# One q load per batch, queries in a permuted order inside blocks, and transposes on halves of the TensorE array

## The chip, the cores and the metric

The kernel runs on one core of a Trainium2 chip. The metric is the device time of one execution in microseconds; the runs shown give a median. A separate profiled execution gives the trace: what each engine (PE = TensorE, ACT = ScalarE, DVE = VectorE, POOL = GpSimd, SP = SyncE) did when, and what it waited for.

## The reference

Two steps, for 8 batches, 8 heads, 576 tokens and head size 64. First an attention over a window of 128 tokens with a distance bias per head, then a token mixer on its output:

```
scores = q @ k.T / 8 ; rel = i - j
scores = where(0 <= rel < 128, scores - slope[h] * |rel|, -1e9)      # slope[h] = 2 ** -(h + 1)
x = softmax(scores) @ v                                    # to [8, 576, 512]
wq, wk = x @ w_q, x @ w_k                                  # [8, 576, 64]
mixed = (wq @ wk.T / 8) @ x
out = maximum(mixed, 0) @ w_out                            # float32
```

Inputs and output are float32; the kernel works in float16 with float32 sums.

## The kernel before, in words

A batch's 576 tokens are four blocks of 128 and a tail of 64. For a batch b the work is made of named operations, and every operation's engine, its place and its PSUM bank are written out in one long text, `ORDER`, in which each word is an operation with its engine (`MUL0.1.0:D`, `XT0.0:P21`). The engines run their own operations in the order of that text. Nothing is planned at run time.

* `Lq`, `Lk`, `Lv` (lines 363 and 380) are loads on POOL's queue that cast to float16; one load is a block of 128 tokens of all heads, in pieces of 256 bytes of float32. `Lt` (line 370) loads the tails of q and k for two batches. The first blocks of batch 0 come over the SP and ACT queues as float32 (`LF`, line 400). `Lw` and `Lwo` load the weights over SP's queue (lines 440 and 448), released by a small DVE operation `wz`.
* `TQ` transposes q and k of a block together on PE (line 234), eight transposes of 128 by 128 into one bank; `ETQ` copies the bank to `qkT`. `TT` and `ETT` do it for the tails.
* `QK` makes the scores of one key block for four heads, in a pair of banks; `EXP` (ACT, line 587) takes the exponential, `MUL` (DVE, line 594) multiplies by the exponential of the bias, a constant tile that also holds the mask. For the last key block, whose queries are 192 + 64 columns, there is a second tile `biasl`.
* `PV` multiplies by v with a column of ones, so that the sums come along; `RC` (line 648) takes the reciprocal and `X` (line 634) scales to x. `PV.4`, `RC.4`, `X.4` are the tail of 64 queries.
* `XT`, `EXT` transpose x and copy it to `xT`; `XTT`, `EXTT` the tails. For each two batches follow `WK`, `WT`, `WQ` (the projections), `G` (wk.T @ x), `MX` with `RM` (mixed, and the relu, lines 770 and 772), and nine output blocks: `OUT`, a copy `EO`, and `DO`, the transfer on SP's queue (lines 832 and 835).

Attention of later batches and the mixer of earlier ones are interleaved by the text. PSUM is four pairs of banks; an operation takes a pair or one bank of it, and holds it until its copy is done. Copies go to ACT (line 238) or DVE (line 240), as the text says. Line 231 is the helper of all matmuls. `WM` are matmuls on zeros at the start.

Of the kernel before, what the change touches and what calls it, by code (L numbers as in the profile page):

```python
# [25 lines left out]
NNAT = 4  # L26
NV = 4
NPT = 5
PTW = 1088
# [4 lines left out]
OSB = 12  # L34
WIDE = ()

WARM = (12, 3, 4, 3, 3, 5,)

ORDER = """
warm:D LF0.0.1.0:A ident:G LF0.0.1.1:A LF0.1.0.1:S ones:D LF0.1.0.0:S Lk0.1:G LF0.0.0.1:S  # L40
LF0.0.0.0:S Lq0.2:G pads:D zeros:D Lt0:G WM.0:P31 TF0.1.1:P00 idh:D TF0.1.0:P01 iota:G Lk0.2:G
wmc:D WM.1:P31 TF0.0.1:P10 EF0.1.0:D EF0.1.1:D mask:G TF0.0.0:P01 EF0.0.1:A Lq0.3:G bias:A
EF0.0.0:D Lk0.3:G WM.2:P31 TJ0.2.0:P00 TJ0.1.1:P01 EJ0.2.0:D QK0.0.1:P1 Lq1.1:G EJ0.1.1:D
QK0.1.1:P0 QK0.0.0:P2 Lv0.0:G EXP0.1.1:A biasl:D TT0:P30 Lq1.2:G TJ0.2.1:P31 EXP0.0.0:A
QK0.1.0:P0 Lk1.1:G EJ0.2.1:D EXP0.0.1:A ETT0:D TJ0.3.0:P31 Lk1.2:G EXP0.1.0:A EJ0.3.0:D ETT1:D
WM.3:P21 TJ0.3.1:P10 Lv0.1:G QK0.2.1:P2 EJ0.3.1:D QK0.2.0:P3 MUL0.1.0:D QK0.3.1:P1 EXP0.2.0:A
Lk1.0:G QK0.3.0:P0 MUL0.0.0:D Lq1.0:G EXP0.2.1:A MUL0.2.0:D MUL0.0.1:D Lk1.3:G EXP0.3.1:A
MUL0.2.1:D PV0.0:P2 Lq1.3:G TQ1.1:P30 EXP0.3.0:A RC0.0:D MUL0.1.1:D TQ1.2:P31 Lv0.2:G ETQ1.1:D
ETQ1.2:A MUL0.3.1:D PV0.1:P0 Lv0.3:G X0.0:D QK1.1.0:P3 Lk2.1:G QK1.1.1:P1 RC0.1:D MUL0.3.0:D
EXP1.1.0:A TQ1.0:P20 Lq2.1:G X0.1:D EXP1.1.1:A ETQ1.0:D XT0.0:P21 Lv1.0:G QK1.0.0:P0 EXT0.0:D  # L50
Lq2.2:G TQ1.3:P20 EXP1.0.0:A MUL1.1.1:D QK1.0.1:P1 PV0.2:P3 Lk2.2:G ETQ1.3:D EXP1.0.1:A
MUL1.0.0:D QK1.2.1:P2 Lv1.1:G QK1.3.1:P0 RC0.2:D EXP1.2.1:A PV0.3:P1 X0.2:D Lq2.3:G RC0.3:D
QK1.2.0:P3 X0.3:D QK1.3.0:P2 Lk2.3:G EXP1.3.0:A MUL1.0.1:D TQ2.1:P10 Lv1.2:G MUL1.1.0:D
EXP1.3.1:A PV1.0:P2 MUL1.2.1:D XT0.1:P11 Lv1.3:G RC1.0:D MUL1.3.0:D EXT0.1:A Lv0.4:G TQ2.2:P00
ETQ2.1:D Lq2.0:G ETQ2.2:A X1.0:D WM.4:P01 PV1.1:P1 MUL1.3.1:D Lv1.4:G EXP1.2.0:A QK2.1.0:P0
QK2.1.1:P2 wz:D RC1.1:D Lw:S Lk2.0:G X1.1:D EXP2.1.0:A TQ2.3:P30 MUL1.2.0:D Lk3.1:G Lwo.1:S
XT1.0:P31 EXP2.1.1:A Lwo.3:S ETQ2.3:D PV1.2:P0 Lt1:G Lwo.2:S PV1.3:P1 EXT1.0:A RC1.2:D Lwo.0:S
X1.2:D PV0.4:P2 RC1.3:D RC0.4:D QK2.2.0:P0 X1.3:D Lq3.1:G EXP2.2.0:A X0.4:D Lk3.0:G WM.5:P30
PV1.4:P1 XT1.1:P31 RC1.4:D X1.4:D QK2.2.1:P0 Lq3.0:G EXT1.1:A XTT0:P30 CWQ:D Lv2.0:G TQ2.0:P10
EXP2.2.1:A EXTT0:D WK0:P31 ETQ2.0:D Lq3.2:G MUL2.1.1:D QK2.0.1:P1 EWK0:A Lk3.2:G QK2.0.0:P0  # L60
MUL2.2.0:D WT0:P30 EXP2.0.1:A WQ0:P31 Lv2.1:G EWT0:D EXP2.0.0:A MUL2.0.1:D G0:P30 CW.1:D EWQ0:A
CW.2:D TT2:P00 MUL2.0.0:D EG0:A Lv2.4:G ETT2:D MX0.4:P3 MX0.1:P1 ETT3:D MX0.0:P2 RMT0:A RM0.1:D
MX0.2:P0 RM1.0:A Lk3.3:G MX0.3:P3 RM0.2:D TQ3.1:P10 RM0.0:A RM0.3:D RM1.2:A Lq3.3:G QK2.3.1:P2
RM1.1:A CW.0:D QK2.3.0:P0 CW.3:D TQ3.0:P30 EXP2.3.1:A Lv2.2:G ETQ3.1:D OUT0.3:P11 ETQ3.0:D
Lk4.2:G EXP2.3.0:A PV2.0:P2 MUL2.1.0:D OUT0.1:P10 Lv3.1:G RM1.3:A RC2.0:D MUL2.3.0:D EO0.3:A
QK3.0.0:P3 Lv2.3:G QK3.0.1:P0 X2.0:D EXP3.0.0:A OUT1.0:P11 MUL2.3.1:D Lv3.0:G EO0.1:A TQ3.2:P20
MUL3.0.0:D OUT0.2:P21 EXP3.0.1:A Lk4.1:G ETQ3.2:D PV2.1:P3 Lq4.2:G EO1.0:A MUL3.0.1:D EO0.2:A
QK3.1.0:P0 QK3.1.1:P1 RC2.1:D Lq4.1:G MUL2.2.1:D EXP3.1.0:A TQ3.3:P20 X2.1:D OUT0.0:P21 Lv3.2:G
EXP3.1.1:A ETQ3.3:D PV2.2:P3 Lq4.0:G MUL3.1.0:D EO0.0:A QK3.2.1:P0 QK3.2.0:P1 RC2.2:D
EXP3.2.1:A Lq4.3:G OUT1.3:P21 X2.2:D MUL3.1.1:D Lv3.3:G EXP3.2.0:A PV2.3:P3 MUL3.2.1:D PV3.0:P0  # L70
OUT1.4:P20 Lk4.3:G EO1.3:A RC2.3:D RC3.0:D X2.3:D Lk4.0:G QK3.3.1:P1 X3.0:D EO1.4:A QK3.3.0:P3
XT2.0:P21 EXP3.3.0:A MUL3.2.0:D Lv3.4:G PV3.1:P0 EXT2.0:D TQ4.2:P20 Lt2:G EXP3.3.1:A MUL3.3.0:D
TQ4.1:P30 XT2.1:P21 RC3.1:D ETQ4.2:A MUL3.3.1:D OUT1.1:P31 Lv4.1:G ETQ4.1:D PV3.2:P1 EXT2.1:D
EO1.1:A Lk5.0:G OUT1.2:P30 RC3.2:D X3.1:D Lv4.0:G PV3.3:P2 X3.2:D EO1.2:A QK4.1.1:P0 Lv4.2:G
RC3.3:D TQ4.3:P30 X3.3:D EXP4.1.1:A QK4.1.0:P1 Lk5.1:G ETQ4.3:D PV2.4:P2 EXP4.1.0:A XT3.0:P31
RC2.4:D TQ4.0:P30 Lq5.0:G X2.4:D EXT3.0:A PV3.4:P0 ETQ4.0:D QK4.2.0:P2 Lq5.1:G XT3.1:P10
RC3.4:D EXP4.2.0:A X3.4:D QK4.2.1:P3 Lq5.3:G TT4:P11 EXT3.1:D EXP4.2.1:A QK4.0.1:P0 Lk5.3:G
XTT2:P20 MUL4.1.1:D WK2:P10 EXP4.0.1:A EXTT2:D Lk5.2:G ETT5:D WT2:P20 ETT4:D EWK2:A Lq5.2:G
MUL4.2.0:D QK4.0.0:P0 QK4.3.1:P3 EWT2:A QK4.3.0:P1 MUL4.2.1:D EXP4.0.0:A WQ2:P21 Lq6.3:G
MUL4.1.0:D EXP4.3.1:A G2:P20 Lv4.3:G MUL4.0.1:D MUL4.0.0:D EWQ2:A Lk6.0:G PV4.2:P3 MUL4.3.1:D  # L80
EG2:A TQ5.1:P21 Lq6.2:G EXP4.3.0:A RC4.2:D X4.2:D MX2.3:P0 TQ5.0:P20 Lv4.4:G RM2.3:A ETQ5.1:D
MX2.0:P3 RM3.3:A Lk6.3:G PV4.1:P1 ETQ5.0:D RM2.0:A MX2.1:P0 MUL4.3.0:D MX2.2:P2 Lk6.2:G RM3.0:A
TQ5.3:P30 RC4.1:D RM2.2:D RM3.2:A TQ5.2:P31 Lq6.0:G RM3.1:A X4.1:D QK5.0.0:P2 ETQ5.2:D Lv5.0:G
EXP5.0.0:A PV4.0:P1 OUT3.3:P01 RC4.0:D ETQ5.3:D Lk6.1:G RM2.1:A QK5.0.1:P2 X4.0:D EO3.3:A
PV4.3:P3 Lq6.1:G MUL5.0.0:D EXP5.0.1:A QK5.2.1:P0 RC4.3:D OUT2.2:P10 Lv5.1:G X4.3:D EXP5.2.1:A
MUL5.0.1:D PV4.4:P2 Lv5.4:G QK5.1.1:P3 EO2.2:A RC4.4:D QK5.1.0:P0 MUL5.2.1:D Lv5.2:G EXP5.1.1:A
XT4.1:P11 DO2.2:S X4.4:D OUT2.0:P10 DO0.3:S Lv5.3:G EXP5.1.0:A EXT4.1:D DO0.1:S TQ6.3:P20 Lt3:G
MUL5.1.1:D DO0.2:S EO2.0:A QK5.3.1:P3 MX2.4:P0 DO1.0:S ETQ6.3:D TQ6.0:P11 EXP5.3.1:A DO0.0:S
TQ6.2:P10 ETQ6.0:D Lq7.1:G RMT2:A QK5.2.0:P2 QK5.3.0:P3 ETQ6.2:D TQ6.1:P11 EXP5.3.0:A Lk7.1:G
MUL5.1.0:D PV5.0:P0 OUT2.1:P10 RC5.0:D EXP5.2.0:A ETQ6.1:D Lk7.0:G PV5.1:P3 X5.0:D Lq7.0:G  # L90
QK6.1.1:P2 EO2.1:A MUL5.2.0:D QK6.0.0:P0 EXP6.1.1:A XT4.0:P11 Lv6.0:G RC5.1:D MUL5.3.1:D
OUT3.0:P10 EXP6.0.0:A X5.1:D Lq7.2:G QK6.0.1:P2 EXT4.0:D QK6.1.0:P3 EXP6.0.1:A XT5.0:P00
MUL5.3.0:D OUT2.3:P11 Lk7.2:G EXT5.0:D EXP6.1.0:A PV5.4:P2 MUL6.0.0:D PV5.2:P0 EO2.3:A RC5.4:D
PV5.3:P3 X5.4:D OUT3.1:P11 EO3.0:A RC5.3:D RC5.2:D X5.3:D QK6.2.1:P2 X5.2:D Lv6.1:G EO3.1:A
QK6.2.0:P3 TT6:P10 EXP6.2.1:A MUL6.1.1:D XTT4:P11 XT5.1:P00 ETT6:D EXP6.2.0:A MUL6.0.1:D
Lk7.3:G OUT3.4:P01 EXT5.1:D QK6.3.0:P3 EXTT4:D QK6.3.1:P2 Lv6.2:G EXP6.3.0:A TQ7.1:P00
MUL6.1.0:D WK4:P11 MUL6.2.0:D Lv6.4:G EXP6.3.1:A MUL6.2.1:D TQ7.0:P30 Lq7.3:G EWK4:A ETQ7.1:D
WT4:P31 WQ4:P20 ETT7:D Lv6.3:G EWT4:A ETQ7.0:D EO3.4:A PV6.0:P1 Lv7.4:G MUL6.3.1:D EWQ4:A
DO3.4:S QK7.0.1:P3 QK7.0.0:P0 RC6.0:D MUL6.3.0:D EXP7.0.1:A DO1.3:S G4:P20 Lv7.0:G DO1.4:S
X6.0:D Lv7.1:G DO1.1:S MUL7.0.1:D TQ7.2:P21 EG4:A DO3.3:S PV6.1:P1 Lv7.3:G EXP7.0.0:A ETQ7.2:D  # L100
DO2.1:S MX4.1:P3 DO1.2:S RC6.1:D QK7.1.1:P2 Lv7.2:G X6.1:D RM5.1:A PV6.2:P0 DO3.0:S EXP7.1.1:A
XT6.0:P31 RC6.2:D X6.2:D MX4.0:P1 RM4.1:A QK7.1.0:P2 EXT6.0:D RM4.0:A MX4.3:P0 TQ7.3:P30
RM5.3:D EXP7.1.0:A OUT3.2:P10 ETQ7.3:D RM4.3:A MX4.2:P2 EO3.2:D RM5.0:A PV6.3:P3 RM4.2:A
MUL7.1.1:D QK7.2.0:P0 RM5.2:A PV6.4:P1 RC6.3:D OUT4.0:P20 X6.3:D EXP7.2.0:A RC6.4:D XT6.1:P21
X6.4:D EO4.0:A MX4.4:P0 QK7.3.1:P3 EXT6.1:D QK7.2.1:P1 RMT4:A DO4.0:S OUT5.1:P20 MUL7.2.0:D
EXP7.2.1:A DO2.0:S DO3.2:S MUL7.1.0:D OUT4.1:P21 EXP7.3.1:A MUL7.0.0:D QK7.3.0:P1 MUL7.2.1:D
EO5.1:A PV7.0:P0 PV7.1:P3 EXP7.3.0:A RC7.0:D DO5.1:S MUL7.3.1:D OUT5.0:P20 DO2.3:S RC7.1:D
EO4.1:A MUL7.3.0:D PV7.2:P1 EO5.0:A X7.1:D OUT5.3:P21 DO5.0:S RC7.2:D X7.2:D PV7.3:P3 EO5.3:A
OUT5.2:P20 X7.0:D RC7.3:D XT7.0:P21 X7.3:D EO5.2:A PV7.4:P0 EXT7.0:D OUT4.3:P10 DO5.2:S RC7.4:D
DO3.1:S X7.4:D XT7.1:P11 EO4.3:A DO4.1:S OUT4.2:P21 EXT7.1:D XTT6:P10 WK6:P11 EXTT6:D WT6:P10  # L110
EWK6:A WQ6:P20 EWT6:A G6:P10 EWQ6:A EO4.2:A OUT5.4:P20 EG6:A DO4.2:S MX6.4:P1 MX6.2:P0 EO5.4:A
MX6.3:P3 RMT6:D RM7.2:A DO5.4:S MX6.0:P2 MX6.1:P1 RM7.3:A DO4.3:S OUT7.4:P01 RM7.1:D RM7.0:A
DO5.3:S RM6.3:A RM6.1:D OUT7.3:P11 EO7.4:A RM6.2:A OUT7.0:P10 DO7.4:S EO7.3:A OUT7.2:P21
# [44 lines left out]
def kernel(  # L158
# [56 lines left out]
    def vtv(b, t):  # L215
        return vt_s[(b // 2) % 2][t][:, b % 2]
# [698 lines left out]
```

## Time and profile before

| what | value |
|---|---|
| median of three runs | 141.13 us (140.97 to 143.18) |
| profiled execution: time | 141.15 us |
| profiled execution: span, first to last instruction | 139.3 us |
| PE, DVE, ACT, POOL busy | 125.9, 114.1, 112.2, 95.6 us |
| granted TensorE clock, mean | 0.987 |
| read from HBM, written | 29.62 MB, 9.44 MB |
| POOL's queue: packets | 109264, 13.77 MB |

A busy time is the union of the engine's instructions; PE's matmuls are pipelined, and their ends are modelled, so a busy PE need not be PE at its peak. A time of the program is 1.8 us longer than the span of its instructions.

### The profile page before, as it was taken

How to read it: one execution, taken by the hardware profiler on the slowest of the kernel's cores; microseconds unless marked ns; L12 is line 12 of the kernel's file. 1: busy time of each engine (PE TensorE's matmuls, PEld its weight loads, DVE VectorE, ACT ScalarE, POOL GpSimd, SP SyncE). 2: the span in 40 equal slices, each digit the busy share in tenths (PEclk: the TensorE clock that was granted, in tenths of full speed). 3: DMA queues.
4: the chain of work that ended last, by engine and by line, in shares of the span. 5: the costliest groups of instructions: out<-in, count | busy, mean ns of one | idle time of the engine just before them, and what ended most of it. 6: DMA issues, size and time to landing. Idle time of an engine off the chain costs nothing.

```text
span 139.3 us, 4479 instructions
## 1 busy us (share of the span) xinstructions
PE 125.9 (90%) x1846; PEld 84.5 (61%) x1846; DVE 114.1 (82%) x254; ACT 112.2 (81%) x165; POOL 95.6 (69%) x118
## 2 busy tenths in 40 slices
PE   6778599879987999999999999999999999999970
PEld 4445486768744566767866477667765656754420
DVE  5657999999996999999999999999998999705000
ACT  3089969898796999868999999978989995279860
POOL 7999999999919999999999999759940000000000
PEclk9999869999999999999999999999999999999999
DMA  4999999999999999999999999999999975505993
GB/s 103 184 155 154 157 153 153 152 150 177 283 184 156 152 155 152 151 153 150 152 151 154 147 172 270 232 202 152 157 171 272 338 274 216 226 5 171 335 355 121
DMA packets 119332, 25.59 MB, mean 184 GB/s; under 512 B 114192, under 2 KB 114192, under 8 KB 119312
## 3 DMA queue, kind: packets, MB, share of 16 engines
q0 software_dynamic: 109264, 13.77, 155.9%
q1 hardware_dynamic: 8992, 11.28, 24.2%
q10 hardware_dynamic: 1056, 0.26, 0.8%
q8 instruction: 14, 0.23, 0.6%
q14 instruction: 6, 0.05, 0.1%
HBM read 29.62 MB, written 9.44 MB: 280 GB/s over the span
## 4 chain that ended last, share of the span: by engine, by line
PE 58%; POOL 22%; DMA 7%; DVE 7%; issue 2%; ACT 1%; ACTq 0%; POOLq 0%
PE pair L231 47%; POOL nat L363 13%; PE pair L234 11%; DMA natt<-in_k_dram 7%; POOL vt L380 6%; DVE pt L594 3%; DVE qkT L240 2%; POOL natt L370 2%; ACT osb L238 1%; DVE x L634 1%; DVE xT L240 0%; DVE rm L772 0%; POOL wm L298 0%; DVE xTt L240 0%; POOL wm L300 0%
## 5 line engine op out<-in xcount | busy, mean ns | idle before, releaser
L587 ACT ACTIVATE pt<-pair 128x1024 f16<-128x1024 f32 x64 | 62.8, 1033 | 4.0 <-PE pair L231 3.6
L380 POOL DMA_DIRECT2D vt<-in_v_dram x40 | 36.9, 976 | 2.6 <-PE pair L231 2.4
L363 POOL DMA_DIRECT2D nat<-in_k_dram x31 | 30.8, 1036 | 3.5 <-DMA nat<-in_k_dram 3.4
L231 PE MATMUL pair<-wout_sb,rm 128*128 128x512 f16 x128 | 31.6, 379 | 0.0
L594 DVE TENSOR_TENSOR pt<-pt,bias 128x1024 f16<-128x1024 f16 x48 | 31.3, 680 | 0.1
L363 POOL DMA_DIRECT2D nat<-in_q_dram x30 | 30.4, 1039 | 0.3 <-DMA vt<-in_v_dram 0.3
L238 ACT COPY osb<-pair 128x512 f32<-128x512 f32 x35 | 20.7, 601 | 7.4 <-PE pair L231 7.2
L231 PEld LDWEIGHTS <-pt 128*128 128x128 f16 x576 | 21.4, 98 | 8.4 <-issue 2.7
L231 PE MATMUL pair<-vt,pt 128*128 128x65 f16 x576 | 24.1, 195 | 2.3 <-ACT pt L587 1.6
L240 DVE COPY qkT<-pair 128x1024 f16<-128x1024 f16 (+1 forms) x38 | 21.7, 591 | 2.6 <-PE pair L231 1.3
L231 PE MATMUL pair<-qkT 64*128 64x256 f16 (+2 forms) x320 | 21.5, 250 | 1.1 <-DVE x L634 0.5
L634 DVE TENSOR_TENSOR x<-pair,inv 128x512 f16<-128x512 f32 x32 | 21.6, 685 | 0.5
L234 PE MATMUL pair<-identh,nat 128*128 128x128 f16 x244 | 19.3, 226 | 1.4 <-ACT pt L587 0.7
L234 PEld LDWEIGHTS <-nat 128*128 128x128 f16 x244 | 15.2, 101 | 5.8 <-issue 3.6
L231 PEld LDWEIGHTS <-rm 128*128 128x128 f16 x128 | 11.1, 97 | 10.6 <-issue 0.8
L231 PEld LDWEIGHTS <-qkT 64*128 64x128 f16 x320 | 11.3, 94 | 7.7 <-issue 3.2
L770 ACT ACTIVATE rm<-pair 128x512 f16<-128x512 f32 x25 | 13.7, 647 | 0.0
L594 DVE TENSOR_TENSOR pt<-pt,biasl 128x1024 f16<-128x1024 f16 x16 | 10.7, 668 | 0.0
L234 PE MATMUL pair<-identh,x 128*128 128x128 f16 x128 | 9.9, 219 | 0.0
L648 DVE RECIPROCAL inv<-pair 128x8 f32<-128x8 f32 (+1 forms) x40 | 7.8, 200 | 1.2 <-PE pair L231 0.8
L234 PEld LDWEIGHTS <-x 128*128 128x128 f16 x128 | 7.6, 98 | 1.7 <-issue 0.8
L240 DVE COPY xT<-pair 128x1024 f16<-128x1024 f16 x12 | 8.2, 687 | 0.4 <-PE pair L234 0.2
(66 smaller groups left out, 116.7 us busy)
## 6 DMA issues: line engine op xcount, KB each, us to landing
out_dram<-osb SPq DMA_DIRECT2D x32, 256.0 KB, 3.0
vt<-in_v_dram POOLq DMA_DIRECT2D x32, 128.0 KB, 5.5
nat<-in_k_dram POOLq DMA_DIRECT2D x31, 128.0 KB, 5.3
nat<-in_q_dram POOLq DMA_DIRECT2D x30, 128.0 KB, 5.1
osb<-in_moe_w_out_dram SPq DMA_DIRECT2D x4, 256.0 KB, 7.2
out_dram<-osb SPq DMA_DIRECT2D x8, 128.0 KB, 3.9
osb<-in_q_dram SPq DMA_DIRECT2D x4, 128.0 KB, 3.8
natt<-in_q_dram POOLq DMA_DIRECT2D x4, 128.0 KB, 7.1
```

The costliest lines, as they stand in the source:

```text
L231: hold(nc.tensor.matmul(*a, **k))
L234: hold(nc.tensor.transpose(*a))
L238: hold(nc.scalar.copy(out_ap, in_ap))
L240: hold(nc.vector.tensor_copy(out=out_ap, in_=in_ap))
L363: return lambda: nc.gpsimd.dma_start(out=natv(b, j, n), in_=(q, k)[j][b, :, P * n:P * n + P, :].transpose([1, 0, 2]))
L370: nc.gpsimd.dma_start(out=natt_s[pr % 2][:, j].rearrange("p e h d -> p (e h) d"), in_=(q, k)[j][2 * pr:2 * pr + 2, :, 512:576, :].rearrang ...
L380: return lambda: nc.gpsimd.dma_start(out=vtv(b, t)[:n, :, 0:D], in_=v[b, :, P * t:P * t + n, :].transpose([1, 0, 2]))
L587: nc.scalar.activation(out=pt[:, 0:1024], in_=two(s.bank).rearrange("p e c -> p (e c)"), func=AF.Exp, scale=SCALE)
L594: ENG2[o.eng].tensor_tensor(out=pt[:, 0:1024], in0=pt[:, 0:1024], in1=bt, op=ALU.mult)
L634: nc.vector.tensor_tensor(out=x[r].rearrange("p (g h d) -> p g h d", g=2, h=4), in0=sums(p)[r, :, :, 0:64], in1=box["inv"][r].unsqueeze(3) ...
L648: nc.vector.reciprocal(out=box["inv"][r], in_=sums(p)[r, :, :, 64])
L770: hold(nc.scalar.activation(out=out_ap, in_=in_ap, func=AF.Relu, scale=WSCALE))
```

## The change

The loads of q: one load per batch, in which a partition holds four neighbouring tokens, so that a piece is 1024 bytes of float32 (`QR = 4`). The queries of a block of 128 therefore stand in another order in everything that follows: token 4 x + r stands at place 32 r + x. The mask and the bias are built for that order, and the relu copy writes its columns back in the order of the tokens. `biasl` goes away: the bias tile gets 384 columns instead of 256, and `MUL` reads two pieces of it.

Transposes of k, x and the tails go through halves of the array (`tp2`): each 128 by 128 transpose is two of 64 rows, which write to the two banks of a pair. q is transposed by head on column halves, two heads side by side. `TQ` and `TK` are separate operations. The tail of 64 queries of `PV` is computed on column halves, heads 0 to 3 on the lower 64 partitions, heads 4 to 7 on the upper, so its reciprocal and scaling work on 128 partitions.

Numbers of buffers change (k tiles for three batches, q for two, v for four, `NPT` 5 to 6, output tiles 12 to 14), the warm-up matmuls stand 23, 2, 5 instead of 12, 3, 4, 3, 3, 5, the last output block is made in two halves of 256 columns, and the whole `ORDER` is another. In it, copies are given to other engines: for instance 6 whole and 2 half output copies to DVE instead of 1, and 13 copies of k and 10 of q to DVE instead of 25 of both.

```diff
-NNAT = 4
+NNAT = 3
+NQ = 2
+QR = 4
-NPT = 5
+NPT = 6
-OSB = 12
+OSB = 14
-WARM = (12, 3, 4, 3, 3, 5,)
+LAST = (7, 3)
+WARM = (23, 2, 5,)
...
+    def tp2(o, m, lo, hi):
+        for r, x in enumerate((lo, hi)):
+            k = slice(64 * r, 64 * r + 64)
+            tp(twoh(o.bank)[:, r, 64 * m:64 * m + 64], x[k], identh[k, k])
...
+    def dma_q(b, r0):
+        return lambda: nc.gpsimd.dma_start(
+            out=natq_s[b % NQ][r0 // QR:P].rearrange("p h r d -> p h (r d)"),
+            in_=q[b, :, r0:512, :].rearrange("h (p r) d -> p h (r d)", r=QR))
...
-            dst = oneh(o.bank).rearrange("p (j c t) -> p j c t", j=2, c=NHP)
-            for j in range(2):
-                for c in range(NHP):
-                    tp(
-                        dst[:, j, c, :],
-                        src[j][:, 2 * c:2 * c + 2, :].rearrange("p a b -> p (a b)"), identh)
+                for c in range(2):
+                    for r in range(QR):
+                        for e in range(2):
+                            dst = oneh(o.bank)[64 * e:64 * e + 64].rearrange(
+                                "p (c t r x) -> p c r t x", c=2, t=4, r=QR)[:, c, r]
+                            tp(dst, natq_s[b % NQ][:, 4 * u + 2 * c + e, r, :], identh)
...
+            def emk(o):
+                for i in range(2):
+                    for c in range(NHP):
+                        x = natk(b, n + i)[:, 2 * c:2 * c + 2, :].rearrange("p a b -> p (a b)")
+                        tp2(o, 2 * c + i, x, x)
...
-            ENG2[o.eng].tensor_tensor(out=pt[:, 0:1024], in0=pt[:, 0:1024], in1=bt, op=ALU.mult)
+            nc.vector.tensor_tensor(out=pv, in0=pv, in1=bt, op=ALU.mult)
...
+            if qt == 4:
+                px = one(o.bank)
+                for h in range(4):
+                    for i, kb in enumerate((3, 4)):
+                        for g in range(2):
+                            mm(px[64 * g:64 * g + 64, 65 * h:65 * h + 65], ptc(kb, 4 * g + h, kb == 4, 64),
+                               vtv(b, kb)[:, 4 * g + h, 0:65], start=(i == 0), stop=(i == 1))
+                return
...
-                    tp(dst[:, c, n, :], x_s[b % NX][2 * i + n][:, P * c:P * c + P], identh)
+                    x = x_s[b % NX][2 * i + n][:, P * c:P * c + P]
+                    tp2(o, 2 * c + n, x, x)
...
-                    relu(o.eng, rm_s[pr % 2][:, db, e, :], two(t.bank)[:, e, :])
+                    relu(o.eng, rm_s[pr % 2][:, d, e, :].rearrange("p (t x r) -> p t r x", t=4, r=QR),
+                         two(t.bank)[:, h, :].rearrange("p (t r x) -> p t r x", t=4, r=QR))
```

## The prediction

> **What bounds the kernel now.** I read the page's busy times and its chain first, then windows cut at two events, and then the DVE and PE timelines.
>
> ```profile
> PE 125.9 (90%) x1846; PEld 84.5 (61%) x1846; DVE 114.1 (82%) x254; ACT 112.2 (81%) x165; POOL 95.6 (69%) x118
> PE 58%; POOL 22%; DMA 7%; DVE 7%; issue 2%; ACT 1%; ACTq 0%; POOLq 0%
> ```
>
> Read alone, these two lines say that TensorE is the bound. I don't follow them, because a pipelined matmul counts as busy while it drains. The DVE timeline gives two events at which the work changes: the first multiplication by the bias (14.32 us) and the end of the last full x tile of batch 7 (117.79 + 0.69 = 118.48 us).
>
> ```profile
> 9.94 0.78 DVE L337 COPY biasl<-bias 128x768 f16<-128x768 f16 x1
> ...
> 14.32 3.10 DVE L594 TENSOR_TENSOR pt<-pt,bias 128x1024 f16<-128x1024 f16 x5
> ...
> 111.49 2.49 DVE L594 TENSOR_TENSOR pt<-pt,bias 128x1024 f16<-128x1024 f16 x4
> ...
> 117.79 0.69 DVE L634 TENSOR_TENSOR x<-pair,inv 128x512 f16<-128x512 f32 x1
> ```
>
> ```profile
> 14.32:118.48 104.16, 98.63 (x1607) 69.31 (x1606) 100.02 (x202) 92.23 (x127) 82.06 (x96) 0.98 2.08 185
> 8.43:14.32 5.89, 4.98 (x67) 3.17 (x65) 5.04 (x12) 5.46 (x10) 5.89 (x8) 1.00 2.42 154
> 118.48:139.30 20.82, 16.41 (x153) 8.23 (x149) 4.70 (x8) 11.89 (x25) 0.00 (x0) 0.99 0.56 203
> ```
>
> In the first window DVE is busy 100.02 of 104.16 us: it stands still for 4.1 us in all, a third of it in one place at 42 us (below). ACT has 11.9 us free there. DVE instructions follow each other more closely than their durations say: in a run of four multiplications (2.49 - 0.68) / 3 = 0.60 us each. So the main phase is a DVE queue of 202 instructions with hardly a hole. In the last window DVE has almost nothing to do, and PE runs to the end:
>
> ```profile
> 122.31 0.32 PE L231 MATMUL pair<-xTt,wqk_sb 128*64 128x64 f16 x8
> 122.46 1.03 PE L231 MATMUL pair<-xT,wqk_sb 128*64 128x512 f16 x8
> 123.36 1.05 PE L231 MATMUL pair<-x,wk 128*64 128x512 f16 x8
> ...
> 127.88 7.07 PE L231 MATMUL pair<-wout_sb,rm 128*128 128x512 f16 x32
> ```
>
> ```profile
> 135.03 0.58 ACT L238 COPY osb<-pair 128x512 f32<-128x512 f32 x1 [0.32 <-PE pair L231]
> ```
>
> Eight output blocks take 7.07 us, 0.86 us each with the overlap; the last copy ends at 135.6, and the last transfer and the close take 3.7 us more. The time is therefore the sum of a start (to the first multiplication), a main phase set by DVE and a tail set by PE.
>
> **The change, part by part.** *PE.* Transposes now go through halves of the array. What whole and half ones cost stands in these rows:
>
> ```profile
> 97.06 0.62 PE L234 MATMUL pair<-identh,nat 128*128 128x128 f16 x8
> 97.52 1.10 PE L231 MATMUL pair<-wqk_sb,xT 128*128 128x64 f16 x32
> ```
>
> ```profile
> 110.16 0.61 PE L234 MATMUL pair<-identh,x 128*128 128x128 f16 x8
> 110.71 0.29 PE L231 MATMUL pair<-wqT,gs 64*128 64x64 f16 x8
> 110.83 0.60 PE L231 MATMUL pair<-qkT 64*128 64x192 f16 x12
> ```
>
> ```profile
> L234 PE MATMUL pair<-identh,nat 128*128 128x128 f16 x244 | 19.3, 226 | 1.4 <-ACT pt L587 0.7 <-DVE x L634 0.3
> L234 PE MATMUL pair<-identh,x 128*128 128x128 f16 x128 | 9.9, 219 | 0.0
> L231 PE MATMUL pair<-vt,pt 128*128 128x65 f16 x576 | 24.1, 195 | 2.3 <-ACT pt L587 1.6 <-DVE qkT L240 0.4
> ```
>
> Eight whole transposes take 97.52 - 97.06 = 0.46 us, 0.0575 each. Eight 64-column matmuls on row halves take 110.83 - 110.71 = 0.12 us, 0.015 each, so a transpose of two halves costs 0.03. A matmul of 512 columns on a column half takes 0.90 / 8 = 0.11 (122.46 to 123.36), so 128 columns cost 0.028. q and k: 244 x 0.0575 = 14.0 us before; after, 224 column halves for q, 32 small ones for batch 0 and 248 row halves for k: 6.3 + 0.5 + 3.7 = 10.5. x: 128 x 0.0575 = 7.4, after 256 x 0.015 = 3.8. The token tails of q, k and x save about 1.3. The last query block of eight batches has 128 matmuls of 65 columns: at the 1.10/32 = 0.03 us of the xT row they cost 3.8 us, on column halves half of that. Together -10.3 us.
>
> Against it: eight transposes ahead of a half-array matmul take 0.55 us (110.16 to 110.71) instead of 0.46, so a change between whole and half array costs 0.09 us. The written order has 95 such changes before and 120 after: +2.3 us, and PE sheds 8.0 us net. The Trainium skill says the same in "TensorEngine Tiling (Array Packing)", Key Properties: a change of tiling mode drains the array. It gives no figure, so by the page alone the sum stays open; by the row the drains leave most of the gain.
>
> In the main phase PE is not what DVE waits for, so I book nothing of these 8 us there; were that cover gone, their worth is that of the first rival.
>
> *DVE, main phase.* Counted from the two orders between the first multiplication and the last full x tile, each operation at its distance in a run: 0.60 us for 1024 f16 or 512 f32 columns, about 0.34 for half of that.
>
> ```profile
> L240 DVE COPY qkT<-pair 128x1024 f16<-128x1024 f16 x25 | 16.8, 681 | 0.4 <-PE pair L234 0.2
> L240 DVE COPY qkT<-pair 128x512 f16<-128x512 f16 x13 | 5.1, 418 | 2.1 <-PE pair L231 1.3 <-PE pair L234 0.6
> L634 DVE TENSOR_TENSOR xtl<-pair,inv 64x512 f16<-64x512 f32 x8 | 5.5, 687 | 0.2
> ```
>
> Copies of q and k 25 to 23: -1.2. Tails of x 7 of 0.60 to 8 of 0.34, since they now fill 128 partitions with 256 columns: -1.5. Relu copies 5 to 3: -1.2. Weight cast, wkt copies and one xTt copy that went to ACT: -1.4. Two more copies of xT: +1.2. One more output copy: +0.6. First-batch copies, pads and a reciprocal that now come after the first multiplication: +1.1. Sum -2.4, so 100.0 becomes 97.6.
>
> *Start.* Four copies for biasl (9.94 to 11.73 us) stand ahead of the first multiplication and go away. ACT gives the first exp result at about 11.5:
>
> ```profile
> 7.55 2.56 ACT L330 ACTIVATE bias<-wm 128x256 f16<-128x256 f32 x8
> 10.52 2.85 ACT L587 ACTIVATE pt<-pair 128x1024 f16<-128x1024 f32 x3 [0.40 <-PE pair L231]
> ```
>
> The eight bias activations grow from 256 to 384 columns (estimate 8 x 0.1 = +0.8 us), but the mask that releases them stands behind about as much POOL work as now, and ACT no longer has a copy of q and k ahead of it. I take 11.6 for the first multiplication, 2.7 us earlier. Then DVE is paced by ACT until batch 0 is through.
>
> *Loads.* Twenty-two of 30 q issues go, 22 x 0.87 us of POOL. That is off the path: loads land as fast as DMA carries them.
>
> ```profile
> 7.06 2.61 POOL nat L363 x3
> GB/s 103 184 155 154 157 153 153 152 150 177 283 184 156 152 155 152 151 153 150 152 151 154 147 172 270 232 202 152 157 171 272 338 274 216 226 5 171 335 355 121
> ```
>
> The plateau of 150 to 157 GB/s is 128 KB per 0.84 us, almost POOL's 0.87. A q load writes 512 KB in pieces of 512 bytes. No row shows such pieces: at the plateau it takes 3.3 us, as its four parts do now; at the 355 GB/s of the output rows 1.5 us. I take 3.0, nearer the plateau, because four times as much is read per piece. The Trainium skill, "DMA: Bandwidth & Descriptors", Specifications, asks for 512 bytes or more per transfer for full rate; by it the 1.5 us would hold, and the 2.5 us that I put below for the wait at the weights would go.
>
> Where loads do decide is where the weights come in:
>
> ```profile
> 31.43 2.06 SPq L448 DMA_DIRECT2D osb<-in_moe_w_out_dram x4
> ```
>
> ```profile
> 32.57 9.87 DMA natt<-in_k_dram
> ...
> 42.93 0.77 DVE qkT L240 x2
> ```
>
> ```profile
> nat<-in_k_dram POOLq DMA_DIRECT2D x31, 128.0 KB, 5.3
> ```
>
> Behind the four weight transfers a k tail needs 9.87 us where a k load takes 5.3 as a rule, and DVE stands for 1.3 us until 42.93. In the new order the weights' turn comes after some 15.5 us of DVE work from the first multiplication, so those four go out at about 29.5 us, 2 us earlier, and behind them stand v 1.2 and k 2.2 and 2.3: the copy of k 2.1 (ETK2.1) waits for them, and all of DVE behind it. I put 2.5 us there, 1 more than now, and DVE's idle time at 5.2 us instead of 4.1.
>
> *Tail.* After the last full x tile the new order has 14 output blocks instead of 12: +1.7 us of PE at 0.86. The PV and transposes there save 0.6; the last block in two halves ends on a copy of half the width and half the transfer: -0.3. Sum +0.8.
>
> *Costs that no row shows.* The multiplication reads the bias in pieces: 0.60, as the 64-column pieces of the 512-column copy keep their rate (418 ns, against 687 for 512 f32); at the f32 rate it would be 0.55 more. The relu writes every fourth element: between nothing and, at half rate, 0.4 us on ACT, which has the room; I take nothing.
>
> **Sum**, against the profiled execution: span 139.3, time 141.15, which is the median (141.13). The last full x tile ends at 11.6 + 97.6 + 5.2 = 114.4 instead of 118.5: -4.1; tail +0.8; sum -3.3 on 141.15, or 137.9; rounded to 138.0.
>
> **Rivals.** *PE was the bound.* For it: the chain's 58%, PE's 90%. Against it: DVE's idle 4.1 us. Then the 8.0 us come off whole: 133.2.
>
> *The time freed turns into waiting for loads.* Everything is as above, but the piece size brings nothing, and v 1.2 and k 2.2 come 2.5 us later still: 140.5. For it: the 9.87 us. Against it: q comes ahead in one piece, and less waits in the queue.
>
> *Slower: the bank pairs run out.* Transposes of k, x and the tails now hold both banks of a pair until copied. Counting a pair as one and a bank as a half, the program takes 180.5 before and 197 after, 9% more, over four pairs. If pairs are what the engines hand round, the main phase grows by up to 9% of 104, +9.5, giving 148.7 with the start's gain and the tail; it decides once DVE idles 11 us in the main phase, and I take 146 for it. Against it: PE's longest waits for a release are few:
>
> ```profile
> PE pair L231 <- ACT pt L587: 1.6, 2, 1.4
> ```
>
> *Slower: the bias in pieces costs DVE its rate.* In the 16 last-block units alone, where the pieces are not neighbours: 16 x 0.55 = +8.8, 146.7; in all 64 it would be some 170.
>
> **How the numbers follow.** A measurement of this kernel tells about 2% from no change, so the lines are 138.3 and 143.9. My forecast has 0.48 with a range of its own of 135.5 to 140.5, the 2.5 us at the weights absent or doubled: 0.30 of it under 138.3, 0.18 above. PE as the bound 0.18, waiting for loads 0.15, bank pairs 0.15, bias pieces 0.04. Faster 0.30 + 0.18 = 0.48; same 0.18 + 0.15 = 0.33; slower 0.19. The range goes from the PE rival, 133.0, to 145.0, short of the dear ends of the slow ones.
>
> **What would show it.** In the profile after: the first multiplication near 11.6 us and the last full x tile near 114.4; DVE idle 5 us between them, its longest wait at 30 to 40 us; qkT copies of k at 0.68 us; half transposes 0.015 us apart; a tail of 21.7 us with PE solid. I am wrong if DVE has large holes and PE has none (first rival), if DVE waits for PE that waits for banks (third), or if the multiplications are longer than 0.69 us (fourth).

## The result, and the profile after

The changed kernel takes 157.58 us (median of four runs, 156.16 to 159.07) against 141.24 us for the kernel before on the same chip: 1.113 times as long, 95% interval 1.103 to 1.123. The prediction was 138.0 us, with a range of 133.0 to 145.0, and it was wrong. Some executions of all these kernels are 2 to 4% longer than their others, mostly at a lower granted clock, and ratios leave those out.

The page of the profiled execution (157.62 us, span 155.8) begins with the busy times; then the clock by slices and the rows of groups that changed. The last number ahead of the second bar is the mean duration of one instruction in ns.

```profile
PE 129.8 (83%) x2310; PEld 82.0 (53%) x2310; DVE 116.5 (75%) x237; ACT 127.6 (82%) x164; POOL 76.6 (49%) x99
PEclk9955999999998799999999955999999986999998
L669 DVE TENSOR_TENSOR pt<-pt,bias 128x1024 f16<-128x1024 f16 x64 | 41.8, 679 | 0.5 <-ACT pt L660 0.5
L878 ACT ACTIVATE rm<-pair 128x512 f16<-128x512 f32 x25 | 30.4, 1392 | 0.5 <-PE pair L243 0.5
L880 DVE TENSOR_SCALAR rm<-pair 128x512 f16<-128x512 f32 x7 | 8.6, 1317 | 0.5 <-PE pair L243 0.5
```

Of the groups of ACT and DVE that both kernels have, those of the relu copy are the only ones whose mean changed much. Before, they were:

```profile
L770 ACT ACTIVATE rm<-pair 128x512 f16<-128x512 f32 x25 | 13.7, 647 | 0.0
L772 DVE TENSOR_SCALAR rm<-pair 128x512 f16<-128x512 f32 x7 | 4.5, 677 | 0.5 <-PE pair L231 0.5
```

A copy that writes every fourth element takes 1392 ns on ACT instead of 647, and 1317 on DVE instead of 677. The eight copies of two batches come together, and there the other engines stop. First the ACT timeline of the changed kernel at the second such place, then DVE's, then PE's; a number in brackets is the engine's idle time before the line, with what ended it.

```profile
84.61 4.72 ACT L878 ACTIVATE rm<-pair 128x512 f16<-128x512 f32 x4
89.07 1.11 ACT L660 ACTIVATE pt<-pair 128x1024 f16<-128x1024 f32 x1
90.07 3.59 ACT L878 ACTIVATE rm<-pair 128x512 f16<-128x512 f32 x3
93.39 2.04 ACT L660 ACTIVATE pt<-pair 128x1024 f16<-128x1024 f32 x2
95.29 1.33 ACT L878 ACTIVATE rm<-pair 128x512 f16<-128x512 f32 x1
```

```profile
89.89 0.69 DVE L257 COPY qkT<-pair 128x1024 f16<-128x1024 f16 x1 [1.90 <-PE pair L246]
...
91.94 2.48 DVE L669 TENSOR_TENSOR pt<-pt,bias 128x1024 f16<-128x1024 f16 x4
97.75 0.69 DVE L257 COPY xT<-pair 128x1024 f16<-128x1024 f16 x1 [3.32 <-PE pair L246]
```

```profile
89.38 0.41 PE L246 MATMUL pair<-identh,natk 64*128 64x64 f16 x16 [2.21 <-ACT rm L878]
...
93.71 3.47 PE L243 MATMUL pair<-wout_sb,rm 128*128 128x512 f16 x8
```

The two long holes of DVE have different ends. Until 89.89 DVE stands 1.90 us for transposes (L246) that themselves wait 2.21 us for a bank that a relu copy still reads. Until 97.75 it stands 3.32 us, and there PE waits for nothing: it makes two output blocks, eight matmuls, in 3.47 us. From 92 to 95 us the granted clock is half of full speed (the column after POOL's):

```profile
92.00:95.00 3.00, 2.33 (x12) 1.04 (x12) 2.42 (x5) 3.00 (x4) 1.15 (x2) 0.50 2.37 149
```

The waits by engine over the whole run (total, times, longest) show the first kind in the middle two rows, and the 3.3 us of the second kind in the last:

```profile
DVE qkT L257 <- PE pair L246: 12.0, 9, 4.3
PE pair L243 <- ACT rm L878: 5.4, 8, 1.1
PE pair L246 <- ACT rm L878: 4.1, 5, 2.2
DVE xT L257 <- PE pair L246: 4.1, 3, 3.3
```

So the chain is relu copy on ACT, bank, transpose on PE, copy on DVE, and behind it comes a stretch of low clock. The last full x tile ends at 131.91 us, not at 114.4:

```profile
11.98:131.91 119.93, 101.78 (x2031) 66.40 (x2028) 99.91 (x205) 109.40 (x134) 65.82 (x78) 0.93 1.60 158
131.91:155.80 23.89, 18.96 (x196) 9.39 (x193) 11.43 (x15) 12.46 (x20) 0.00 (x0) 0.98 0.56 199
```

In this view of windows the columns are the stretch, its length, the busy times of PE, PEld, DVE, ACT and POOL, the granted clock, the DMA share and GB/s. DVE is busy 99.91 of 119.93 us: 20.0 us of idle time instead of 4.1. The main theory (A) was that the write of every fourth element is all of the loss. Its rivals: (B) pairs of banks run out because transposes by halves hold both banks; (C) loads and the lower clock (0.93 in the first window, 0.98 before) are a cause and not an effect.

### The profile page after: what moved, and what is told of

Its sections match the earlier page's. It is cut to its first block, busy times and chain, and to the rows that moved or that the text cites. A ratio compares the mean times of both kernels' runs of the same rounds, so it can differ in the third digit from the quotient of the medians.

```text
span 155.8 us, 5383 instructions
## 1 busy us (share of the span) xinstructions
PE 129.8 (83%) x2310; PEld 82.0 (53%) x2310; DVE 116.5 (75%) x237; ACT 127.6 (82%) x164; POOL 76.6 (49%) x99
## 3 DMA queue, kind: packets, MB, share of 16 engines
q1 hardware_dynamic: 9136, 11.28, 21.7%
## 5 line engine op out<-in xcount | busy, mean ns | idle before, releaser
L669 DVE TENSOR_TENSOR pt<-pt,bias 128x1024 f16<-128x1024 f16 x64 | 41.8, 679 | 0.5 <-ACT pt L660 0.5
L243 PE MATMUL pair<-wout_sb,rm 128*128 128x512 f16 (+1 forms) x132 | 33.9, 398 | 1.1 <-ACT rm L878 1.0
L878 ACT ACTIVATE rm<-pair 128x512 f16<-128x512 f32 x25 | 30.4, 1392 | 0.5 <-PE pair L243 0.5
L384 POOL DMA_DIRECT2D natk<-in_k_dram x31 | 27.9, 909 | 4.7 <-DMA natt<-in_q_dram 2.9
L243 PE MATMUL pair<-vt,pt 128*128 128x65 f16 (+1 forms) x576 | 23.6, 197 | 3.1 <-DVE xtl L727 0.7
L243 PEld LDWEIGHTS <-pt 128*128 128x128 f16 (+1 forms) x576 | 19.9, 102 | 9.9 <-issue 6.0
L246 PE MATMUL pair<-identh,natq 128*64 128x128 f16 (+1 forms) x256 | 10.2, 229 | 1.2 <-ACT rm L878 0.7
L246 PEld LDWEIGHTS <-natq 128*64 128x64 f16 (+1 forms) x256 | 8.3, 118 | 3.3 <-issue 2.8
L246 PE MATMUL pair<-identh,natk 64*128 64x64 f16 x248 | 7.3, 198 | 3.1 <-ACT rm L878 2.4
L880 DVE TENSOR_SCALAR rm<-pair 128x512 f16<-128x512 f32 x7 | 8.6, 1317 | 0.5 <-PE pair L243 0.5
```

Source lines behind the costliest of these rows:

```text
L243: hold(nc.tensor.matmul(*a, **k))
L246: hold(nc.tensor.transpose(*a))
L384: return lambda: nc.gpsimd.dma_start(out=natk(b, n), in_=k[b, :, P * n:P * n + P, :].transpose([1, 0, 2]))
L669: nc.vector.tensor_tensor(out=pv, in0=pv, in1=bt, op=ALU.mult)
L878: hold(nc.scalar.activation(out=out_ap, in_=in_ap, func=AF.Relu, scale=WSCALE))
L880: hold(nc.vector.tensor_scalar(out=out_ap, in0=in_ap, scalar1=0.0, scalar2=WSCALE, op0=ALU.max, op1=ALU.mult))
```

## Experiments

### The relu copy reads with gaps and writes side by side

```diff
-  relu(o.eng, rm[...].rearrange("p (t x r) -> p t r x", t=4, r=QR),
-       two(t.bank)[:, h, :].rearrange("p (t r x) -> p t r x", t=4, r=QR))
+  relu(o.eng, rm[...].rearrange("p (t x r) -> p t x r", t=4, r=QR),
+       two(t.bank)[:, h, :].rearrange("p (t r x) -> p t x r", t=4, r=QR))
```

> The changed kernel, but the relu copy reads its PSUM bank in the order of the tokens (each float32 128 bytes from the one before) and writes its f16 row side by side; the result is the same. If only a write with gaps is dear: relu copies 0.65 to 0.70 us and 136 to 140 us in all. If a read with gaps costs as much as a write with gaps: relu copies 1.3 to 1.4 us and 155 to 159 us, as the changed kernel. Theory B (banks): 146 or above whatever the copies take.

Measured: 141.11 us, ratio to the kernel before 0.996 (0.9925 to 1.0004). All that differs from the changed kernel is which side of the copy has the gaps, and 16.5 us are gone. That is 1 us above the 136 to 140 of the first theory and 5 below the 146 of theory B. The rows of groups, the same eight output matmuls as above, and the windows of this kernel:

```profile
L878 ACT ACTIVATE rm<-pair 128x512 f16<-128x512 f32 x25 | 13.7, 623 | 0.9 <-PE pair L243 0.9
L880 DVE TENSOR_SCALAR rm<-pair 128x512 f16<-128x512 f32 x7 | 4.6, 684 | 0.9 <-PE pair L243 0.9
```

```profile
84.96 1.90 PE L243 MATMUL pair<-wout_sb,rm 128*128 128x512 f16 x8
```

```profile
11.72:116.72 105.00, 95.13 (x2033) 63.18 (x2029) 97.84 (x205) 96.03 (x134) 66.06 (x78) 0.98 1.83 180
116.72:138.50 21.78, 18.16 (x194) 9.27 (x192) 9.37 (x15) 10.22 (x20) 0.00 (x0) 0.99 0.63 224
```

A read of PSUM in steps of 128 bytes costs nothing here (623 ns on ACT and 684 on DVE, against 647 and 677 side by side). Theory B falls: the transposes by halves are all there, and DVE's idle time is 105.00 - 97.84 = 7.2 us. Theory C falls too: the clock is back at 0.98 with the same loads. The dips of the changed kernel after 40 us (the 87, the second 55 and the 86 of its PEclk row; 0.66 from 90 to 100 us) come at the three places of the dear copies, and this kernel has none after 20 us. So in this pair they are part of the price and not a cause of their own. How much of the 16.5 us goes through them was not measured apart; PE is busy 129.8 us in the changed kernel and 122.3 here, with the same 2310 matmuls.

Against the changed kernel the main phase is 14.9 us shorter and the tail 2.1, while ACT's busy time falls by 13.4 and 2.2: in this pair the time follows the extra ACT time nearly one to one.

### The price in the kernel before

```diff
-  relu(o.eng, rm_s[pr % 2][:, db, e, :], two(t.bank)[:, e, :])
+  relu(o.eng, rm_s[pr % 2][:, db, e, :].rearrange("p (t x r) -> p t r x", t=4, r=4),
+       two(t.bank)[:, e, :].rearrange("p (t r x) -> p t r x", t=4, r=4))
```

> The kernel before, with nothing changed but the relu copy, which writes every fourth element as in the changed kernel (its output rows come in another order). Theory A: the 32 relu copies take 1.39 us on ACT and 1.32 on DVE, 25 x 0.74 + 7 x 0.64 = 23 us more of copying, and the time is 148 to 160. Theory B (the copy matters only where banks are short): the copies grow by as much, but hide, and the time is under 145.

```profile
L770 ACT ACTIVATE rm<-pair 128x512 f16<-128x512 f32 x25 | 30.4, 1390 | 0.0
L772 DVE TENSOR_SCALAR rm<-pair 128x512 f16<-128x512 f32 x7 | 8.6, 1306 | 1.6 <-PE pair L231 1.6
```

Its waits have PE behind the relu copy as well:

```profile
PE pair L231 <- ACT rm L770: 9.1, 12, 1.6
```

158.02 us against 141.35 us, ratio 1.117 (1.109 to 1.124): in the old order, with none of the rest of the change, the same edit costs 16.7 us. Theory A holds from both sides.

### The order of the tokens restored at the query projection

```diff
-  cp(o.eng, wqT_s[pr % 2][rows, 0:512], one(t.bank)[rows])
+  cp(o.eng, wqT_s[pr % 2][rows, 0:512].rearrange("p (t x r) -> p t x r", t=4, r=QR),
+     one(t.bank)[rows].rearrange("p (t r x) -> p t x r", t=4, r=QR))
...
-  relu(o.eng, rm[...].rearrange(...), two(t.bank)[:, h, :].rearrange(...))
+  relu(o.eng, rm_s[pr % 2][:, d, e, :], two(t.bank)[:, h, :])
```

> The changed kernel, but the order of the tokens is restored earlier: the copy of the query projection (one for two batches, 4 in the program, all on ACT) reads its PSUM bank in the order of the tokens, and the 32 relu copies write side by side; the result is the same. Theory A: relu copies 0.65 us; the 4 copies take 0.65 to 1.4 us each; 136 to 141 us. Theory B: 146 or above. Theory C: above 150.

Its four runs took 140.85, 143.14, 145.13 and 145.21 us; only the first can be compared, and it lies within the 136 to 141 of theory A. The copies of the query projection on ACT took 603 ns. (The expectation has all four on ACT; the last is on DVE.)

```profile
L255 ACT CAST wqT<-pair 128x512 f16<-128x512 f32 x3 | 1.8, 603 | 0.8 <-PE pair L243 0.8
```

It agrees with theory A, and it shows a second place where the order can be put back with no dear copy. One run can't rank it against the first.

### The rows put in place by the output transfer

```diff
-  nc.sync.dma_start(out=out[b, P * st:P * st + P, :], in_=osb)
+  nc.sync.dma_start(out=out[b, P * st:P * st + P, :].rearrange("(x r) d -> r x d", r=QR), in_=osb)
```

> The changed kernel, but the relu copies write their 512 columns side by side, and the output transfers put the rows back in the order of the tokens (each row stays one piece of 2048 bytes). Theory A (the relu copy's write of every fourth element is the whole loss): relu copies take 0.65 us on ACT and 0.68 on DVE again instead of 1.39 and 1.32, the holes of DVE at 44 to 53, 84 to 97 and 118 to 134 us go, the last full x tile ends at 113 to 116, and the time is 136 to 140. Theory B (pairs of banks run out because the transposes by halves hold both banks of a pair; the relu copy only adds to it): PE still waits for banks, DVE idles 11 us or more in the main phase, and the time stays at 146 or above. Theory C (loads and the clock: the late natural tiles and the dips of the granted clock are the cause): the granted clock stays near 0.93 and the time above 150.

187.64 us, ratio 1.326 (1.319 to 1.333): none of the theories named this. The relu copies were short (624 ns on ACT), but the transfers piled up. Windows late in this run, when nothing but output moves:

```profile
160.00:180.00 20.00, 0.00 (x0) 0.00 (x0) 0.00 (x0) 0.00 (x0) 0.00 (x0) 0.50 0.26 102
```

The DMA share is 0.26, about what four of 16 engines would give, at 102 GB/s. The pattern's outermost dimension was 4. The Trainium skill, "DMA: Bandwidth & Descriptors", Why a DMA increments its semaphore by 16 and not by 1, says that a transfer is spread over the largest number of engines, up to 16, that divides the outermost dimension of both sides; the 0.26 agrees. To see whether that was all, each transfer was cut into four:

```diff
+  for r in range(QR):
+      nc.sync.dma_start(out=out[b, P * st:P * st + P, :].rearrange("(x r) d -> r x d", r=QR)[r],
+                        in_=osb[32 * r:32 * r + 32])
```

> As the run whose output transfers put the rows in the order of the tokens (187.6 us), but each transfer is cut into four of 32 partitions, each of 32 rows of 2048 bytes. If the one transfer was slow because its outermost dimension of 4 spread it over a quarter of the DMA engines: the four together go at the 250 to 380 GB/s of the other output transfers and the time falls to 140 to 147, with SP issuing 4 times as many. If rows scattered over DRAM are slow: still above 180.

```profile
140.00:155.00 15.00, 0.00 (x0) 0.00 (x0) 0.42 (x1) 0.00 (x0) 0.00 (x0) 0.50 0.54 146
```

168.62 and 171.39 us in two runs, 146 GB/s at a share of 0.54: better, but neither forecast. The timeline of SP's queue shows what holds it:

```profile
147.74 13.26 SPq L984 DMA_DIRECT2D out_dram<-osb  x28
```

From 90 to 165 us SP issues these transfers with hardly a pause, here one every 0.47 us, and 64 KB in 0.47 us is about 139 GB/s. An issue takes 0.43 us (median) and carries a quarter of what one of 0.40 us carries in the kernel with the gaps on the reading side. Each piece lands 1.7 us after its issue (median), so none of them piles up, though its rows are as scattered as before. This run is bound by the number of its issues, which the expectation mentions and does not price.

### Which gaps are dear

All 32 copies got one of 16 forms, each on a line of its own: eight for the write (one side by side, seven with gaps) and the same eight for the read.

```diff
+  if f == 1: hold(act(out=o.rearrange("p (a b c) -> p b a c", a=4, b=4), in_=...))     # runs of 32
+  if f == 2: hold(act(out=o.rearrange("p (x r) -> p r x", r=2), in_=...))              # step 2; 3, 4, 5: steps 4, 8, 16
+  if f == 6: hold(act(out=o.rearrange("p (x r a) -> p r x a", r=2, a=2), in_=...))     # runs of 2; 7: runs of 4
...
```

> The changed kernel with all 32 relu copies on ACT, in 16 forms, two of each; the columns of the output come in another order for most of them, so only the durations are read. Eight forms write with gaps and read side by side, eight the other way round: side by side; runs of 32 elements; steps of 2, 4, 8 and 16 elements; runs of 2 and of 4 elements with as large a gap behind each. Theory P (the write loses its rate when it can't put two neighbours in one word): steps of 2, 4, 8 and 16 all take about 1.39 us, runs of 2 and more 0.65. Theory G (the write loses its rate with the distance of the gap, from 8 bytes on): a step of 2 elements (4 bytes) takes 0.65, steps of 4 and more 1.39. Theory D (the number of dimensions of the write is what costs): runs of 32 are as dear as step 4. Reads: 0.65 in all eight forms, as a step of 32 float32 cost nothing in the earlier run. The Trainium skill, SBUF - State Buffer, DMA Layer, states that two hits in a line of 16 bytes keep full rate; by it a step of 4 elements of 2 bytes would take 0.65 and only 8 and 16 be dear, which the 1.39 us of the changed kernel speak against.

Each line is one form on ACT: count, then the shortest, mean and longest duration in ns, in the order side by side, runs of 32, steps of 2, 4, 8 and 16, runs of 2 and of 4.

```profile
L889 ACT ACTIVATE rm<-pair x2: 592/808/1025, 56.8 to 119.6; 128x512 f16<-128x512 f32 x2
L891 ACT ACTIVATE rm<-pair x2: 618/655/692, 46.4 to 120.4; 128x512 f16<-128x512 f32 x2
L893 ACT ACTIVATE rm<-pair x2: 804/806/807, 53.9 to 117.1; 128x512 f16<-128x512 f32 x2
L895 ACT ACTIVATE rm<-pair x2: 1322/1488/1653, 49.2 to 125.6; 128x512 f16<-128x512 f32 x2
L897 ACT ACTIVATE rm<-pair x2: 2522/2547/2572, 50.6 to 117.7; 128x512 f16<-128x512 f32 x2
L899 ACT ACTIVATE rm<-pair x2: 2368/2397/2426, 47.4 to 120.9; 128x512 f16<-128x512 f32 x2
L901 ACT ACTIVATE rm<-pair x2: 650/808/965, 52.6 to 116.6; 128x512 f16<-128x512 f32 x2
L903 ACT ACTIVATE rm<-pair x2: 603/618/632, 46.9 to 125.1; 128x512 f16<-128x512 f32 x2
```

A copy that follows a dear one can look longer (965 on L901, just behind the 2.57 us of L897), so the shortest is taken as the form's own. The eight forms of the read had means of 612 to 667 ns. Theory D falls (runs of 32 have as many dimensions and cost nothing), P and G are each half right: 0.80 at a step of 4 bytes, 1.32 at 8, 2.4 to 2.5 at 16 and at 32. That grows as the elements in one stretch of 16 bytes become fewer (four, two, one, one) and then stops. The Trainium skill, "SBUF — State Buffer", Specifications (TRN2), has lines of 16 bytes of which two hits keep full rate (the expectation gives another section for it); here a step of 8 bytes, two elements to a line, takes 2.2 times as long as side by side (1322 against 592), so the measurement decides. On DVE:

> The same 16 forms with all 32 relu copies on DVE (columns of the output in another order; only the durations are read). On ACT the isolated copies took 0.59 us side by side, 0.62 in runs of 32, 0.80 at a step of 2 elements, 1.32 at 4, 2.5 at 8 and 2.4 at 16, 0.65 in runs of 2, 0.60 in runs of 4, and 0.61 to 0.67 for all reads with gaps. Theory M (the price is the store's, whichever engine writes): 0.68, 0.68, 0.8 to 0.9, 1.32, 2.4 and 2.4 on DVE too, runs and reads at 0.68. Theory N (each engine's own): DVE writes at a step of 8 and 16 for the 1.32 us that it takes at 4.

```profile
L926 DVE TENSOR_SCALAR rm<-pair x2: 717/722/726, 54.3 to 121.4; 128x512 f16<-128x512 f32 x2
L928 DVE TENSOR_SCALAR rm<-pair x2: 1266/1278/1291, 48.5 to 131.4; 128x512 f16<-128x512 f32 x2
L930 DVE TENSOR_SCALAR rm<-pair x2: 2402/2414/2426, 50.2 to 122.6; 128x512 f16<-128x512 f32 x2
L936 DVE TENSOR_SCALAR rm<-pair x2: 681/681/681, 45.2 to 130.8; 128x512 f16<-128x512 f32 x2
```

Steps of 2, 4 and 8, and runs of 4: nearly the same prices on the other engine (a step of 16 takes 2.29 us), so theory M holds but for the step of 2, which is cheaper on DVE. The price goes with the write, on both engines tried.

### Is it the time on ACT, or its place?

Three kernels put about the same extra time, 5.3 to 5.6 us of ACT, into the kernel whose relu writes side by side: as dear writes in one group of batches, as a burst of extra activations in that place, and spread.

```diff
+  # one group: batches 2 and 3 (pr == 1) write "p t r x" as in the changed kernel
+  # burst, spread: after op.emit(op), for the op names in EXTRA
+  if op.name in EXTRA:      # burst: RM2.0 to RM3.3; spread: EXP3.0.0, EXP3.2.0 to EXP6.2.0
+      nc.scalar.activation(out=extra, in_=extra, func=AF.Relu, scale=WSCALE)
```

> The kernel whose relu reads with gaps and writes side by side (141.1 us), but the 8 relu copies of batches 2 and 3, all on ACT, write every fourth element as in the changed kernel. If each dear copy costs its extra ACT time in full, 8 x 0.66 = 5.3 us: 145.5 to 147.5. If the loss comes only from three such bouts together: under 143.5.

> As the spread run, but the 8 extra activations stand one behind each of the 8 relu copies of batches 2 and 3, whose own duration stays 0.65 us. Theory S (the relu's longer time on ACT, in that place, is all that costs): 145.5 to 147.5, as the run with 8 dear writes. Theory W (the write itself disturbs others, by SBUF or by holding the bank): clearly less than that run, under 144.

> The kernel whose relu writes side by side (141.1 us), with 8 extra activations of 736 columns in SBUF on ACT, 0.66 us each, one after the exponential of key blocks 0 and 2 of batches 3 to 6: the same 5.3 us of ACT work as in the run beside it, but spread, and no bank is held by it. Theory R (my prediction's: ACT has room, some 9 us in the main phase; the place is what costs): 141 to 142.5. Theory L (ACT's time is on the path everywhere): 145 to 147.

One group of dear writes: 145.75 us, the median of three runs (145.33 to 147.01; a fourth took 149.90), 4.6 us above 141.1, inside the range for a price paid in full. Burst: 148.4 us, 7.3 above, and above the 145.5 to 147.5 of theory S. The extra activations followed the copies by 0.70 us each (83.77 to 84.47), so 5.6 us of that is their time. Where the other 1.7 us come from stays open. They would fit a hole of DVE of 2.12 us ahead of the first of them (0.51 in the kernel without them), where PE was busy without a break but at a granted clock of 0.65; why the clock fell there isn't known, and it falls again behind the burst, to 0.80 from 90 to 100 us. From the timeline of ACT, the timeline of DVE and the windows of that run:

```profile
83.77 0.81 ACT L1031 ACTIVATE extra<-extra 128x736 f16<-128x736 f16 x1
84.47 0.59 ACT L881 ACTIVATE rm<-pair 128x512 f16<-128x512 f32 x1
```

```profile
44.33 0.42 DVE L259 COPY qkT<-pair 128x512 f16<-128x512 f16 x1 [2.12 <-PE pair L248]
```

```profile
40.00:44.00 4.00, 4.00 (x43) 1.77 (x42) 1.96 (x4) 2.23 (x4) 3.20 (x4) 0.65 1.83 186
```

Theory W falls: plain ACT time in that place costs at least as much as the dear write. Spread: 144.67 and 144.83 us (two more runs took 147.29 and 148.10), 3.6 above. Theory R, which was my prediction's, falls as well: ACT had no such room. The window from 60 to 70 us, first without the spread activations:

```profile
60.00:70.00 10.00, 8.92 (x213) 6.44 (x209) 9.66 (x21) 9.68 (x14) 8.68 (x11) 1.00 2.36 159
```

and then with them:

```profile
60.00:70.00 10.00, 8.59 (x196) 6.11 (x190) 8.50 (x19) 9.93 (x14) 8.41 (x10) 1.00 2.37 158
```

ACT goes from 9.68 to 9.93, full, and DVE falls from 9.66 to 8.50. Theory L is nearer, though it asked for 145 to 147. Six of the eight start between 54 and 82 us, where ACT and DVE are nearly full. So extra time on ACT costs in either place, and less where it is spread.

## Why the prediction was wrong, and where it was right

*The step that failed* is the last of the costs "that no row shows": "The relu writes every fourth element: between nothing and, at half rate, 0.4 us on ACT, which has the room; I take nothing." Both halves were wrong. The size is 745 ns on ACT (1392 against 647) and 640 on DVE; the upper bound of 0.4 was too low because I allowed for no more than half the rate. The cover was wrong too: I took ACT's 11.9 free us from a mean over the main phase. Where the relu copies stand it isn't there, and the profile of before said so, ahead of any change. At the three places of its relu copies in the main phase ACT is busy 27.3 of 28 us:

```profile
43.00:51.00 8.00, 7.70 (x89) 4.40 (x85) 8.00 (x16) 7.87 (x13) 8.00 (x10) 1.00 2.36 152
74.00:84.00 10.00, 9.88 (x149) 6.41 (x148) 9.81 (x20) 9.74 (x16) 10.00 (x14) 1.00 2.24 161
104.00:114.00 10.00, 9.99 (x149) 6.01 (x146) 9.22 (x18) 9.69 (x16) 0.00 (x0) 1.00 1.22 305
```

The relu copies stand ahead of exponentials in ACT's queue and keep their banks, so each longer copy delays MUL and the transposes, and a stretch of low clock follows (0.50 at the second place). The 21 of them that ACT has in the main phase add 13.4 us to its busy time there (109.40 against 96.03), more than even the mean's room. In all, the term that I put at nothing is worth 16.5 us. The Trainium skill speaks against the step as well: "Vector Engine (DVE) Microarchitecture Reference", Measured stream behaviour on trn2, gives 1.05 ns a column for neighbours and 1.71 to 2.5 when each element is written apart from the last, for 4-byte elements, which is 0.66 to 1.45 more. On DVE the 1317 ns here are 1.25 ns a column more than the 677, so this trace agrees.

*What was right* can be read from the kernel with the gaps on the reading side, since it is the change without that step.

| step | forecast | measured there |
|---|---|---|
| first multiplication | 11.6 us | 11.72 us |
| DVE work in the main phase | 97.6 us | 97.84 us |
| DVE idle there | 5.2 us | 7.16 us |
| last full x tile | 114.4 us | 116.72 us |
| tail | 21.7 us | 21.78 us |
| time | 138.0 us | 141.11 us (profiled execution 140.28) |

Of the 2.4 us between the forecast span of 136.1 and its 138.5, 2.0 are DVE idle time. The 1 us more at the weights didn't come: from 30 to 50 us DVE idles 1.98 us, and 1.97 in the kernel before. Other holes did, most of them under 0.6 us: 1.24 us from the first multiplication to 20 us, and 2.94 us from 80 us to the last full x tile, where the kernel before has 0.07 and 1.57. In the 30 us from 50 DVE is busy 29.10 and ACT 29.06 (29.54 and 27.79 before):

```profile
50.00:80.00 30.00, 28.27 (x619) 19.62 (x617) 29.10 (x59) 29.06 (x40) 24.95 (x30) 1.00 2.14 166
```

So the change gives ACT more work in the main phase (96.03 us against 92.23) and DVE less (97.84 against 100.02), and the 2.2 us that it saves on DVE are lost again in 3.0 us of further waiting: without the dear write it is worth nothing that can be measured (0.996, interval to 1.0004). That a fuller ACT is what makes DVE wait is argued, not shown; the spread activations show only that ACT had no room left there. The tail came out as a sum; its three terms were not measured apart. Transposes by halves: in the PE timeline of that kernel 16 of them take 117.22 - 116.97 = 0.25 us, 0.016 each, as forecast (0.015).

```profile
116.97 0.41 PE L246 MATMUL pair<-identh,x 64*128 64x64 f16 x16
117.22 0.28 PE L246 MATMUL pair<-identh,xtl 64*128 64x64 f16 x8
```

The rivals: PE was not the bound (its transposes became cheaper and the time did not fall). The bias in pieces costs nothing: MUL takes 679 ns, as before. Pairs of banks did show the sign that I had given ("if DVE waits for PE that waits for banks"), but the sign belonged to another cause: the banks were held by the relu copy, and with that copy short they sufficed. The wait for loads was not needed to explain anything. What a q load takes by itself was not read off a row, so neither the 3.0 us nor the 1.5 us of the forecast is confirmed.

## What to carry to other kernels

When an access pattern changes, price the side that writes to SBUF by itself, and above all where 16-bit elements are written 8 bytes or more apart; the same permutation on the reading side of a copy from PSUM was free here. Don't take an engine's room from a mean over a long phase: read the stage in which the extra work stands, and ask what queues behind it. An unknown that is multiplied by 32 needs a bound from a row, and "at most half the rate" is not one.

## What the runs showed of the hardware that I had not expected

* Writing f16 to SBUF from ACT: 0.59 us for 512 columns side by side, 0.80 at a step of 4 bytes, 1.32 at 8, 2.4 to 2.5 at 16 and 32; DVE 0.72, 1.27 and 2.40 at 4, 8 and 16. Runs of 2 (0.65 on ACT) and of 4 elements are free or nearly so.
* Reading float32 from PSUM with steps of up to 128 bytes cost nothing (623 ns on ACT, 684 on DVE).
* Output transfers whose outermost dimension was 4 ran at a DMA share of 0.26 and 102 GB/s, and made the kernel 46.5 us longer than the one with the gaps on the reading side.
* Cut into four of 64 KB, these transfers took SP's queue 0.47 us each, and the issuing held the kernel at 168.62 us.
* Behind the long relu copies, where PE had waited for banks, the granted clock fell to 0.50 for some us, and eight matmuls took 3.47 us instead of 1.90.
